# Spreading the queries' reciprocals over their heads' rows: sixteen matmuls with a 0/1 matrix, or transfers through DRAM

## The chip, the cores and the metric

The kernel runs on one core of a Trainium2 chip. The core has a matrix engine (TensorE, PE in the profile), a vector engine (VectorE, DVE), a scalar engine (ScalarE, ACT), GpSimd (POOL) and SyncE (SP). Each engine works through its own list of instructions in order and waits on semaphores where it needs another's result. Transfers are issued here by SP and POOL (a few by ACT) and run on sixteen shared DMA engines. SBUF is the on-chip memory of 128 partitions; PSUM holds what PE writes.

The metric is the device time of one launch in microseconds (us), as the median of several runs. Before the change it is 2350.26 us, the median of 3 runs from 2349.44 to 2350.53.

## The reference

Two branches read the same input `x` of 2048 rows by 512, and a sigmoid gate mixes them. Branch A is linear attention with 32 heads of 16 columns. Branch B is a mixture of eight experts; all eight are taken, each weighted by a softmax.

```python
def _A_ref(x, wqkv, wo):
    H = 32; Dh = D // H
    ...
    phi = lambda t: jnp.where(t > 0, t + 1, jnp.exp(t)) + 1e-6
    pq, pk = phi(q), phi(k)
    kv = jnp.einsum("bhsd,bhse->bhde", pk, v)
    z = jnp.einsum("bhsd->bhd", pk)
    num = jnp.einsum("bhqd,bhde->bhqe", pq, kv)
    den = jnp.einsum("bhqd,bhd->bhq", pq, z)[..., None] + 1e-6
    o = num / den
    return ... o.reshape(B, S, D) @ wo

def _B_ref(x, w_gate, w1, w2):
    ...
    for e in range(E):
        h = _silu(xf @ w1[e]) @ w2[e]
        out = out + w * h

g = _sigmoid((x * gate_w).sum(-1, keepdims=True))
return g * a + (1 - g) * b
```

What matters here is `den`: one sum for each query and head. Each of the 16 columns of a head in `pq` is divided by it. The kernel divides `pq` ahead of the product with `kv`, and folds the gate `g` into the same factor.

## The kernel before, in words

**Tiling.** A value is held as a high and a low float32r part, and a product is three matmuls (`mm3`, lines 57 to 60: high by high, high by low, low by high). The large products go through seven smaller ones each (a Strassen-like scheme), named P1 to P7. The rows come in two halves `h` of 1024, and each half in two blocks `j` of 512 columns. A tile is 128 partitions by 512.

**Parts and ticks.** `m.parts` (line 112) lists the parts in the order in which their second products run: eight experts of the first half, four of the second, the attention's output projection of the first half (`A[0]`), four more experts of the second half, and the attention's second half (`A[1]`). The main loop, `for u in range(LAG + NTICK)` (line 1096), runs one *tick* per turn. In a tick PE does six matmuls of the first products for group `g` (`up`) and six of the second products, `LAG` = 58 ticks behind (`tick(n)` with `n = u - LAG`), so a tick is twelve matmuls of 128x512. The position in a group is `k`, 0 to 6. Everything else is hung into the ticks by hand: each engine's list is in the order in which this loop emits it.

**Order inside a tick.** `other()` comes ahead of the first products and emits preparation of weights, the low halves of hidden tiles (up to three ticks ahead of their matmuls), their high halves, and `queries_first`. `mid()` comes behind the first products and emits `tick(n)` and `queries_last`. The sums `s<-c` (line 690, at k = 5) and `s<-a` (line 696, at k = 6) on DVE empty the PSUM banks `c` and `a`. PSUM tag `a` has two banks; at k = 0 of the next group one of them gets the new `a`, while the old one gets one more product (`a<-n6h`, k = 1).

**The queries' passes.** `m.beside` (line 123) names four parts, and beside each of them one pass `i` runs, for half `h` and block `j` with `h, j = divmod(i, 2)`. Its step `s` is the tick counted from the part's start.

- s = -3, `queries_load`: for even `i` a raw tile `az` is taken, which holds `z` (the keys' sums by head), `spread` (the 0/1 matrix) and `un` (two 128x512 places). SP loads `zcd`, `spd` and the four 128x512 tiles of `pq` (DRAM `pqd`).
- s = 0 to 3: ACT and DVE split each `pq` tile into `un`; PE multiplies by `z` into PSUM `dn`, which gives the 32 sums of each query.
- s = 4 to 9: the high and low sums are added, DVE takes reciprocals in four pieces, and multiplies by the gate (line 982). `Q.r` is 32 x 512.
- s = 10: ACT and DVE split `Q.r` into 64 rows of `un` (lines 984 and 985). POOL has set the rest to zero (line 977).
- s = 14 to 17: PE multiplies by `spread`, one matmul per tile (line 1000), into PSUM `n` with tag `a`; this repeats each head's row over its 16 partitions.
- s = 15 to 18: DVE multiplies each `pq` tile by it (line 988), and SP stores it (line 989).

The matrix `spread` is built on POOL early in the kernel (`bands`, t = 7, lines 438 to 444) and kept in DRAM as `spd`.

Of the kernel before, what the change touches and what calls it, by code (L numbers as in the profile page):

```python
# [10 lines left out]
F32 = mybir.dt.float32  # L11
F32R = mybir.dt.float32r
AF = mybir.ActivationFunctionType
ALU = mybir.AluOpType
AX = mybir.AxisListType

P = 128
S = 2048
D = 512
F = 1792  # L20
E = 8
DH = 16
NH = D // DH
KT = D // P
TB = 512
# [12 lines left out]
def f32(ap):  # L38
    return ap.bitcast(F32)


@with_exitstack
def gated_mix_kernel(ctx: ExitStack, tc: tile.TileContext, xT, x, wk, wv, wqkv_q, wo, wm, out):
    nc = tc.nc
    PS = bass.MemoryType.PSUM

    const = ctx.enter_context(tc.tile_pool(name="const", bufs=1))
    xpool = ctx.enter_context(tc.tile_pool(name="xpool", bufs=14))
    w1p = ctx.enter_context(tc.tile_pool(name="w1p", bufs=1))
    psum = ctx.enter_context(tc.tile_pool(name="psum", bufs=1, space=PS))  # L50
    dram = ctx.enter_context(tc.tile_pool(name="dram", bufs=1, space=bass.MemoryType.DRAM))
    ctx.enter_context(tc.manual_schedule())

    m = SimpleNamespace(nc=nc, tc=tc, const=const, xpool=xpool, w1p=w1p, psum=psum, v=nc.vector,
                        xT=xT, x=x, wk=wk, wv=wv, wq=wqkv_q, wo=wo, wm=wm, out=out)

    def mm3(ps, wh, wlo, xh, xl, start, stop):
        nc.tensor.matmul(ps, wh, xh, start=start, stop=False, skip_group_check=True)  # L58
        nc.tensor.matmul(ps, wh, xl, start=False, stop=False, skip_group_check=True)  # L59
        nc.tensor.matmul(ps, wlo, xh, start=False, stop=stop, skip_group_check=True)  # L60

    def act_copy(dst, src, scale=1.0, bias=0.0):
        nc.scalar.activation(dst, src, AF.Copy, scale=scale, bias=bias)  # L63

    def ps_tile(name, tag, bufs=None):
        return psum.tile([P, TB], F32, name=name, tag=tag, bufs=bufs or {"a": 2, "b": 1, "c": 1, "dn": 4}[tag])

    m.mm3, m.act_copy, m.ps_tile = mm3, act_copy, ps_tile


    def phi_first(dst, src):
        nc.scalar.activation(dst, src, AF.Exp)
        nc.scalar.activation(src, src, AF.Relu)

    def phi_last(dst, src):
        nc.vector.scalar_tensor_tensor(dst, dst, 1.0, src, op0=ALU.min, op1=ALU.add)

    def phi(dst, src):
        phi_first(dst, src)
        phi_last(dst, src)  # L80

    def eps_high(h, d):
        act_copy(h, d, bias=EPS)

    def eps_low(lo, d, h):
        nc.vector.scalar_tensor_tensor(lo, d, EPS, f32(h), op0=ALU.add, op1=ALU.subtract)

    m.phi, m.phi_first, m.phi_last, m.eps_high, m.eps_low = phi, phi_first, phi_last, eps_high, eps_low
    m.ident = const.tile([P, P], F32, name="ident")


    def x_tile(name, tag="x"):
        return xpool.tile([P, 2, TB], F32R, name=name, tag=tag, bufs=14 if tag == "x" else 2)

    m.x_tile = x_tile
    m.XO = [[None] * 7, [None] * 7]
    m.xstash = dram.tile([7, 2, P, 2 * TB], F32, name="xstash")
    m.w2stash = [dram.tile([P, 2, D], F32, name=f"w2stash{i}") for i in range(7 * (E * NPAIR + 2) // 2)]
    m.wgtd = dram.tile([E + 1, S], F32, name="wgtd")
    m.acct = dram.tile([2, 2, KT, P, TB], F32, name="acct")  # L100
    m.pqd = dram.tile([2, 2, KT, P, TB], F32, name="pqd")
    m.wpd = [dram.tile([P, D], F32, name=f"wpd{c}") for c in range(KT)]
    m.zcd = dram.tile([P, KT * 2 * NH], F32, name="zcd")
    m.spd = dram.tile([P, KT * P], F32, name="spd")

    X = [[SimpleNamespace(e=e, h=h, n=NPAIR) for e in range(E)] for h in range(2)]
    A = m.A = [SimpleNamespace(e=E, h=h, n=2) for h in range(2)]
    M = E // 2  # L110

    m.parts = [*X[0], *X[1][:M], A[0], *X[1][M:], A[1]]
    at = 0
    for part in m.parts:
        part.t0, at = at, at + 7 * part.n
    m.NTICK = at
    m.groups = [(part, q) for part in (A[0], *X[0], *X[1][:M], A[1], *X[1][M:]) for q in range(part.n)]
    m.NG = len(m.groups)
    for part in m.parts:
        part.gs = [g for g, (p, _) in enumerate(m.groups) if p is part]  # L120
    m.G1 = X[1][0].gs[0]

    m.beside = [*X[1][:2], *X[1][M:M + 2]]

    misc = ExitStack()
    m.misc = misc.enter_context(tc.tile_pool(name="misc", bufs=1, side="right"))


    def pad(pool):
        nc.gpsimd.memset(pool.tile([P, 24], F32, name="pad", tag="pad", bufs=1), 0.0)  # L130

    m.pad = pad
    weights(m)
    keys(m)
    experts(m, misc)


# [181 lines left out]
def keys(m):  # L319
# [106 lines left out]
    def band(t, pattern, channel):  # L426
        nc.gpsimd.memset(t, 1.0)
        nc.gpsimd.affine_select(out=t, in_=t, compare_op=ALU.is_ge, fill=0.0, base=0,
                                pattern=pattern, channel_multiplier=channel)
        nc.gpsimd.affine_select(out=t, in_=t, compare_op=ALU.is_ge, fill=0.0, base=DH - 1,  # L430
                                pattern=[[-a, n] for a, n in pattern], channel_multiplier=-channel)

    def bands(t):
        if t == 5:
            band(mask.rearrange("p (b e) -> p b e", e=DH), [[-DH, P // DH], [0, DH]], 1)
        elif t == 6:
            band(maskh, [[P, KT], [-DH, NH]], 1)
        elif t == 7:

            spread = m.w1p.tile([P, 2, D], F32, name="spread", tag="ws", bufs=2)[:, 0]  # L440
            nc.gpsimd.memset(spread[2 * NH:], 0.0)
            for i in range(2):
                band(spread[i * NH:(i + 1) * NH].rearrange("p (c f) -> p c f", c=KT), [[P, KT], [1, P]], -DH)
            nc.gpsimd.dma_start(m.spd, spread)

    pk = {}

# [130 lines left out]
def experts(m, misc):  # L578
# [369 lines left out]

    Q = SimpleNamespace()

    def queries_load(i):
        if i % 2 == 0:
            Q.az = m.raw_tile(f"az{i}", F32R)
            Q.z = Q.az[:, :2 * KT * NH].rearrange("p (c f) -> p c f", c=KT)
            Q.spread = Q.az[:, 2 * KT * NH:2 * KT * NH + D].rearrange("p (c f) -> p c f", c=KT)
            Q.un = Q.az[:, 2 * KT * NH + D:2 * KT * NH + 3 * D].rearrange("p (j t) -> p j t", j=2)
            nc.sync.dma_start(f32(Q.az[:, :2 * KT * NH]), m.zcd)
            nc.sync.dma_start(f32(Q.az[:, 2 * KT * NH:2 * KT * NH + D]), m.spd)  # L960
        Q.d = m.raw_tile(f"pq{i}").rearrange("p (c t) -> p c t", c=KT)
        for c in range(KT):
            nc.sync.dma_start(Q.d[:, c], m.pqd[i // 2, i % 2, c])

    def queries_first(i, s):
        h, j = divmod(i, 2)
        if 0 <= s < KT:
            m.eps_high(Q.un[:, 0], Q.d[:, s])
            m.eps_low(Q.un[:, 1], Q.d[:, s], Q.un[:, 0])
        elif s == 4:  # L970
            r = Q.r = out_tile(f"r{i}")[:NH]
            Q.gate = out_tile(f"rg{i}")[:NH]
            at = (2 * h + j) * TB
            nc.sync.dma_start(Q.gate, m.wgtd[E:E + 1, at:at + TB].to_broadcast([NH, TB]))
            act_copy(r, Q.ps[NH:2 * NH], bias=EPS)
            v.tensor_add(r, Q.ps[:NH], r)
            nc.gpsimd.memset(f32(Q.un[2 * NH:, 0]), 0.0)
        if 5 <= s < 9:
            r = Q.r[:, (s - 5) * P:(s - 4) * P]
            v.reciprocal(r, r)  # L980
        elif s == 9:
            v.tensor_mul(Q.r, Q.r, Q.gate)
        elif s == 10:
            act_copy(Q.un[:NH, 0], Q.r)
            v.tensor_sub(Q.un[NH:2 * NH, 0], Q.r, f32(Q.un[:NH, 0]))
        if 15 <= s < 15 + KT:
            d = Q.d[:, s - 15]
            v.scalar_tensor_tensor(d, d, EPS, Q.ps, op0=ALU.add, op1=ALU.mult)
            nc.sync.dma_start(m.pqd[h, j, s - 15], d)

    def queries_last(i, s):
        if 0 <= s < KT:
            if s == 0:
                Q.ps = ps_tile(f"dn{i}", "a")
            for j in range(2):
                nc.tensor.matmul(Q.ps[:2 * NH, :], Q.z[:, s], Q.un[:, j], start=(s == 0 and j == 0),
                                 stop=(s == KT - 1 and j == 1))
        elif 14 <= s < 14 + KT:
            Q.ps = ps_tile(f"n{i}_{s}", "a")
            nc.tensor.matmul(Q.ps, Q.spread[:, s - 14], Q.un[:, 0], start=True, stop=True)  # L1000


    def load_query(part, i):
# [227 lines left out]
```

## Time and profile before

| | |
|---|---|
| median of 3 runs | 2350.26 us (2349.44 to 2350.53) |
| the profiled execution, its own time | 2350.77 us |
| its span, first to last instruction | 2349.1 us |
| mean granted clock of PE | 0.999 |
| DMA, mean over the span | 218 GB/s, 513.23 MB |
| HBM read, written | 343.43 MB, 163.52 MB |

The profile is of one execution. A row of a group gives the source line, the engine, the operation, the tile written and the tiles read, the shapes and the count, and then the duration in ns as least, median and greatest, with the start of the first and the last instruction. A row of the timeline begins with the start and the duration in us; brackets at its end give the idle time before it and what ended that. "A <- B: x, y, z" in a list of waits says that A waited for B for x us in total, y times, at most z. PEld is the load of a matmul's stationary operand, which overlaps the matmuls. Line numbers are those of the kernel before.

### The profile page before, as it was taken

What the parts mean: (1) busy time and instruction counts of PE and PEld (TensorE: products, weight loads), DVE (VectorE), ACT (ScalarE), POOL (GpSimd) and SP (SyncE); (2) the same over time, 40 slices, a digit from 0 to 9 for tenths busy, and PEclk for the clock granted to TensorE, in tenths of its full rate; (3) what the DMA queues carried; (4) which work ended last, traced back from release to release, by engine and by line L of the source; (5) the groups of instructions that cost most, each with busy time, mean ns of one, the idle gap of its engine ahead of it and who ended that gap; (6) DMA issues with size and microseconds to landing.
All of it is one profiled execution on the core that took longest, in us unless ns stands there. A gap on an engine that the chain in (4) does not pass through costs nothing.

```text
span 2349.1 us, 31301 instructions
## 1 busy us (share of the span) xinstructions
PE 2338.4 (100%) x10492; PEld 1935.4 (82%) x10492; DVE 1811.9 (77%) x3102; ACT 1419.3 (60%) x2655; POOL 158.7 (7%) x222
## 2 busy tenths in 40 slices
PE   9999999999999999999999999999999999999999
PEld 8877888888888888888888888888888888888887
DVE  6798888888888888888677768776676777766666
ACT  6686666666666656666555555555565655555553
POOL 2101000000000000000000000000011000000101
PEclk9999999999999999999999999999999999999999
DMA  7898888988889898988845455654556655555566
GB/s 225 239 311 249 264 288 249 278 263 267 268 267 275 256 290 252 271 269 262 287 144 170 152 172 153 182 186 144 163 166 188 182 150 174 162 166 166 165 220 207
DMA packets 299345, 513.23 MB, mean 218 GB/s; under 512 B 24352, under 2 KB 193840, under 8 KB 298800
## 3 DMA queue, kind: packets, MB, share of 16 engines
q1 hardware_dynamic: 274992, 464.10, 59.8%
q0 software_dynamic: 23344, 46.49, 10.8%
q8 instruction: 82, 1.34, 0.2%
q10 hardware_dynamic: 848, 0.66, 0.1%
q14 instruction: 79, 0.65, 0.1%
HBM read 343.43 MB, written 163.52 MB: 216 GB/s over the span
## 4 chain that ended last, share of the span: by engine, by line
PE 97%; DVE 1%; DMA 1%; issue 0%; ACT 0%; POOL 0%; DVEq 0%; ACTq 0%; POOLq 0%
PE p L58 16%; PE p L60 16%; PE p L59 16%; PE a L58 8%; PE a L60 8%; PE a L59 8%; PE c L59 4%; PE c L58 4%; PE c L60 4%; PE b L60 2%; PE b L59 2%; PE b L58 2%; PE g L451 2%; DMA w2stash<-w 1%; PE y L58 1%; PE y L60 1%
## 5 line engine op out<-in xcount | busy, mean ns | idle before, releaser
L58 PE MATMUL p<-ho,w 128*128 128x512 f32 x1620 | 631.4, 390 | 0.8 <-DVE d L844 0.6
L60 PE MATMUL p<-ho,w 128*128 128x512 f32 x1620 | 630.3, 389 | 0.0
L59 PE MATMUL p<-ho,w 128*128 128x512 f32 x1620 | 630.3, 389 | 0.0
L760 DVE TENSOR_TENSOR ho<-s,ho 128x512 fp32r<-128x512 f32 x784 | 537.2, 686 | 71.2 <-ACT ho L63 67.6
L63 ACT ACTIVATE ho<-s 128x512 fp32r<-128x512 f32 x784 | 487.3, 623 | 21.0 <-PE p L60 8.5
L58 PEld LDWEIGHTS p<-ho,w 128*128 128x128 f32 x1620 | 304.0, 188 | 66.7 <-ACT p L63 1.8
L60 PEld LDWEIGHTS p<-ho,w 128*128 128x128 f32 x1620 | 304.2, 188 | 63.2
L59 PEld LDWEIGHTS p<-ho,w 128*128 128x128 f32 x1620 | 304.1, 188 | 63.0
L63 ACT ACTIVATE o<-rs 128x512 fp32r<-128x512 f32 x224 | 129.1, 576 | 172.7 <-PE a L60 111.7
L690 DVE TENSOR_TENSOR s<-c,s 128x512 f32<-128x512 f32 x116 | 80.2, 692 | 188.6 <-PE c L60 178.7
L63 ACT ACTIVATE o<-rm 128x512 fp32r<-128x512 f32 x240 | 137.5, 573 | 99.8 <-PE a L60 77.4
L63 ACT ACTIVATE s<-a 128x512 f32<-128x512 f32 x116 | 69.5, 599 | 146.9 <-PE a L60 140.3
L63 ACT ACTIVATE ws<-rm 128x512 fp32r<-128x512 f32 x203 | 114.7, 573 | 66.2 <-DMA w2stash<-ws 59.3
L619 ACT ACTIVATE s<-s 128x512 f32<-128x512 f32 x224 | 138.7, 619 | 9.9 <-DVE s L696 6.6
L619 ACT ACTIVATE s<-b 128x512 f32<-128x512 f32 x112 | 67.2, 600 | 112.4 <-PE b L60 100.3
L205 DVE TENSOR_TENSOR o<-rm,o 128x512 fp32r<-128x512 f32 x180 | 122.9, 683 | 0.1
L205 DVE TENSOR_TENSOR o<-rs,o 128x512 fp32r<-128x512 f32 x168 | 114.5, 681 | 0.6 <-ACT o L63 0.6
L219 DVE TENSOR_TENSOR ws<-rm,ws 128x512 fp32r<-128x512 f32 x154 | 105.5, 685 | 0.5 <-ACT ws L63 0.5
L696 DVE TENSOR_TENSOR s<-a,s 128x512 f32<-128x512 f32 x116 | 80.0, 689 | 32.8 <-PE a L60 32.5
L63 ACT ACTIVATE b<-a 128x512 f32<-128x512 f32 x116 | 67.1, 579 | 58.1 <-PE a L60 58.0
L63 ACT ACTIVATE s<-c 128x512 f32<-128x512 f32 x116 | 69.0, 595 | 25.6 <-PE c L60 25.6
L815 POOL DMA_DIRECT2D acct<-c x30 | 25.6, 854 | 794.8 <-DVE c L809 779.8
(321 smaller groups left out, 4540.5 us busy)
## 6 DMA issues: line engine op xcount, KB each, us to landing
w<-w2stash SPq DMA_DIRECT2D x403, 512.0 KB, 4.0
w2stash<-ws SPq DMA_DIRECT2D x357, 256.0 KB, 4.2
rm<-wm SPq DMA_DIRECT2D x228, 256.0 KB, 5.2
rs<-wm SPq DMA_DIRECT2D x108, 256.0 KB, 4.0
wb<-wgtd SPq DMA_DIRECT2D x16, 512.0 KB, 5.2
acct<-c POOLq DMA_DIRECT2D x30, 256.0 KB, 5.6
acct<-d POOLq DMA_DIRECT2D x30, 256.0 KB, 5.5
acct<-k POOLq DMA_DIRECT2D x30, 256.0 KB, 5.5
```

The costliest lines, as they stand in the source:

```text
L58: nc.tensor.matmul(ps, wh, xh, start=start, stop=False, skip_group_check=True)
L59: nc.tensor.matmul(ps, wh, xl, start=False, stop=False, skip_group_check=True)
L60: nc.tensor.matmul(ps, wlo, xh, start=False, stop=stop, skip_group_check=True)
L63: nc.scalar.activation(dst, src, AF.Copy, scale=scale, bias=bias)
L205: v.tensor_sub(two(o, 1), src, f32(two(o, 0)))
L219: v.tensor_sub(two(w, 1), src, f32(two(w, 0)))
L451: nc.tensor.matmul(ps, xk((0, 0, 1)[j], tb, k, tt * P, (tt + 1) * P), gw[g][:, (0, 1, 0)[j], k, :], start=(k == 0 and j == 0), stop=(k == ...
L619: nc.scalar.activation(dst, src, AF.Silu)
L690: v.tensor_add(sn[g, 2], bank[g, "c"], sn[g, 2])
L696: v.tensor_add(sn[g, 3], bank[g, "a"], sn[g, 3])
L760: v.tensor_sub(h[1], s, f32(h[0]))
L815: nc.gpsimd.dma_start(m.acct[part.h, j, dt], s, accum_op=ALU.add)
```

## The change

The sixteen matmuls with the 0/1 matrix go, and with them the matrix, its DRAM tensor, the split of `Q.r`, and the memset. In their place `Q.r` is written to a DRAM tensor `rd` by POOL at s = 9, and at s = 10 POOL issues three loads that read each head's row 16 times into 16 partitions. Tile c of the four needs heads 8c to 8c + 7. The loads go into a fresh place `more` of `az` and into the two places of `un`; the fourth goes into `more` again, issued at s = 15 behind the multiplication that reads the first. DVE's multiplications at s = 15 to 18 read these places instead of PSUM.

```diff
-    m.spd = dram.tile([P, KT * P], F32, name="spd")
+    m.rd = dram.tile([2, 2, NH, TB], F32, name="rd")
...
-        elif t == 7:
-
-            spread = m.w1p.tile([P, 2, D], F32, name="spread", tag="ws", bufs=2)[:, 0]
-            nc.gpsimd.memset(spread[2 * NH:], 0.0)
-            for i in range(2):
-                band(spread[i * NH:(i + 1) * NH].rearrange("p (c f) -> p c f", c=KT), [[P, KT], [1, P]], -DH)
-            nc.gpsimd.dma_start(m.spd, spread)
...
-            Q.spread = Q.az[:, 2 * KT * NH:2 * KT * NH + D].rearrange("p (c f) -> p c f", c=KT)
-            Q.un = Q.az[:, 2 * KT * NH + D:2 * KT * NH + 3 * D].rearrange("p (j t) -> p j t", j=2)
+            Q.un = Q.az[:, 2 * KT * NH:2 * KT * NH + 2 * D].rearrange("p (j t) -> p j t", j=2)
+            more = Q.az[:, 2 * KT * NH + 2 * D:2 * KT * NH + 3 * D]
+            Q.by = [f32(t) for t in (more, Q.un[:, 0], Q.un[:, 1], more)]
             nc.sync.dma_start(f32(Q.az[:, :2 * KT * NH]), m.zcd)
-            nc.sync.dma_start(f32(Q.az[:, 2 * KT * NH:2 * KT * NH + D]), m.spd)
...
+        def spread(c):
+            heads = m.rd[h, j, c * P // DH:(c + 1) * P // DH]
+            nc.gpsimd.dma_start(Q.by[c], heads[:, None, :].to_broadcast([P // DH, DH, TB]))
...
-            nc.gpsimd.memset(f32(Q.un[2 * NH:, 0]), 0.0)
...
         elif s == 9:
             v.tensor_mul(Q.r, Q.r, Q.gate)
+            nc.gpsimd.dma_start(m.rd[h, j], Q.r)
         elif s == 10:
-            act_copy(Q.un[:NH, 0], Q.r)
-            v.tensor_sub(Q.un[NH:2 * NH, 0], Q.r, f32(Q.un[:NH, 0]))
+            for c in range(KT - 1):
+                spread(c)
         if 15 <= s < 15 + KT:
             d = Q.d[:, s - 15]
-            v.scalar_tensor_tensor(d, d, EPS, Q.ps, op0=ALU.add, op1=ALU.mult)
+            v.scalar_tensor_tensor(d, d, EPS, Q.by[s - 15], op0=ALU.add, op1=ALU.mult)
             nc.sync.dma_start(m.pqd[h, j, s - 15], d)
+            if s == 15:
+                spread(KT - 1)
...
-        elif 14 <= s < 14 + KT:
-            Q.ps = ps_tile(f"n{i}_{s}", "a")
-            nc.tensor.matmul(Q.ps, Q.spread[:, s - 14], Q.un[:, 0], start=True, stop=True)
```

## The prediction

> **What bounds the kernel now.** I read first the page's head, its clock row and the chain that ended last.
>
> ```profile
> span 2349.1 us, 31301 instructions
> PE 2338.4 (100%) x10492; PEld 1935.4 (82%) x10492; DVE 1811.9 (77%) x3102; ACT 1419.3 (60%) x2655; POOL 158.7 (7%) x222
> PEclk9999999999999999999999999999999999999999
> PE 97%; DVE 1%; DMA 1%; issue 0%; ACT 0%; POOL 0%; DVEq 0%; ACTq 0%; POOLq 0%
> ```
>
> The last row is the point: TensorE (PE) carries 97% of the chain, and its clock is granted throughout. The busy share alone proves little, because the matmuls overlap. So I asked next what PE waited for over the whole span, and how much work each engine has in the stretches where the changed code runs (four passes, near 1260, 1400, 1840 and 1980 us).
>
> ```profile
> PE a L58 <- DVE s L696: 3.9, 2, 3.2
> PE idle L515 <- POOL ones L423: 1.4, 1, 1.4
> PE p L58 <- DVE d L844: 0.6, 1, 0.6
> ```
> ```profile
> 400.00:600.00 200.00, 200.00 (x884) 165.62 (x883) 168.98 (x281) 128.01 (x242) 11.86 (x14) 1.00 0.89 269
> 1300.00:1312.00 12.00, 12.00 (x55) 9.94 (x54) 10.51 (x19) 6.64 (x13) 0.00 (x0) 1.00 0.48 168
> 1420.00:1440.00 20.00, 20.00 (x90) 16.56 (x89) 15.76 (x28) 12.85 (x24) 0.00 (x0) 1.00 0.32 107
> 1860.00:1880.00 20.00, 20.00 (x90) 16.56 (x89) 15.73 (x30) 13.06 (x24) 0.00 (x0) 1.00 0.40 132
> 2000.00:2020.00 20.00, 20.00 (x90) 16.55 (x89) 15.21 (x28) 13.02 (x25) 0.00 (x0) 1.00 0.39 122
> ```
>
> All waits of PE add up to 5.9 us, and none names a tile of the change. The columns of the second fence are the stretch, its length, then busy time and count of PE, weight loads, DVE, ACT and POOL, the clock, the DMA share and GB/s. PE is full in each stretch, with a matmul every 200/884 = 0.226 us; DVE and ACT have room, POOL does nothing, and the DMA engines are less than half used. So a PE instruction taken from one of these passes should shorten the whole program by its place in the stream, and work on other engines is free until it makes PE wait.
>
> **The change: PE's part.** Sixteen products (`n<-az`, four in each of four passes) go.
>
> ```profile
> L1000 PE MATMUL n<-az x16: 389/389/389, 1300.4 to 2022.5; 128*128 128x512 f32 x16
> L988 DVE SCALAR_TENSOR_TENSOR pq<-pq,n x16: 678/682/689, 1301.4 to 2023.8; 128x512 f32<-128x512 f32 x16
> L63 ACT ACTIVATE az<-r x4: 615/615/615, 1287.2 to 2000.5; 32x512 fp32r<-32x512 f32 x4
> L985 DVE TENSOR_TENSOR az<-r,az x4: 680/681/682, 1287.9 to 2001.1; 32x512 fp32r<-32x512 f32 x4
> L977 POOL MEMSET az<- x4: 521/521/521, 1270.5 to 1983.8; 64x512 f32 x4
> L86 DVE SCALAR_TENSOR_TENSOR az<-pq,az x16: 683/692/693, 1259.4 to 1981.2; 128x512 fp32r<-128x512 f32 x16
> ```
> ```profile
> 1300.19 0.39 PE L60 MATMUL p<-ho,w 128*128 128x512 f32 x1
> 1300.42 0.39 PE L1000 MATMUL n<-az 128*128 128x512 f32 x1
> 1300.65 0.39 PE L58 MATMUL b<-n2h,o 128*128 128x512 f32 x1
> 1303.37 0.39 PE L1000 MATMUL n<-az 128*128 128x512 f32 x1
> ```
>
> A product shows 0.389 us, but the next matmul starts 0.23 us after it, as in the rest of the stream. Its price on the path is that distance: 16 x 0.226 = 3.62 us. The bounds are zero (another engine would have held PE anyway) and these 3.62 us; 16 x 0.389 = 6.2 us is no bound, since the overlap isn't given back. I take 3.62: there is no gap before or behind the products. In the order in which the two programs' instructions stand, these 16 are all that PE's stream loses, and nothing changes places around them. The Trainium skill's page "TensorE: Matmul & The Clock Gate" (section "Wait — 56ns, not 53.3ns?") gives 215.7 ns from start to start for 512 columns at full clock; by it the sum would be 3.45 us. The trace's distance is longer, and the trace decides.
>
> **What goes from other engines.** Each pass loses a 0.615 us copy on ACT, a 0.681 us subtraction on DVE and a 0.52 us memset on POOL. PE's full stream covers them (DVE is busy 15 to 16 us of 20 there), so they are worth nothing; uncovered they would bring at most 4 x (0.615 + 0.681) = 5.2 us. At the start POOL no longer builds the matrix of zeros and ones.
>
> ```profile
> 50.99 0.52 POOL L441 MEMSET spread<- 64x512 f32 x1
> 56.51 0.60 POOL L444 DMA_DIRECT2D spd<-spread  x1 [0.30 <-POOL spread L430]
> ```
> ```profile
> 187.82 0.70 PE L58 MATMUL a<-t6h,o 128*128 128x512 f32 x1 [3.15 <-DVE s L696]
> ```
>
> That is 6 us of POOL and one 256 KB write, while PE doesn't wait; zero. The nearest wait of PE behind it is the 3.15 us one above, 130 us later. SP loses two loads of the matrix; also zero. The multiplications that read `n` read SBUF instead of PSUM: the nearest row, L86, has both sources in SBUF and takes 0.692 against 0.682 us, 0.16 us in sum on DVE, covered by PE.
>
> **What is added: two transfers in a row ahead of DVE.** Per pass POOL writes the 32 x 512 reciprocals to DRAM, waits for that to land, and issues three loads of 256 KB that repeat each row for 16 partitions. The fourth load goes into the first one's place, so it is issued only after the first multiplication. The clock of the first pass, in the rows of before:
>
> ```profile
> 1284.82 0.67 DVE L982 TENSOR_TENSOR r<-r,rg 32x512 f32<-32x512 f32 x1
> 1301.38 0.68 DVE L988 SCALAR_TENSOR_TENSOR pq<-pq,n 128x512 f32<-128x512 f32 x1
> 1308.17 0.69 DVE L690 TENSOR_TENSOR s<-c,s 128x512 f32<-128x512 f32 x1 [0.74 <-PE c L60]
> 1310.59 0.68 DVE L988 SCALAR_TENSOR_TENSOR pq<-pq,n 128x512 f32<-128x512 f32 x1
> 1311.18 0.68 DVE L696 TENSOR_TENSOR s<-a,s 128x512 f32<-128x512 f32 x1
> ```
> ```profile
> 1314.93 0.39 PE L58 MATMUL a<-n6h,o 128*128 128x512 f32 x1
> ```
> ```profile
> L1012 POOL DMA_DIRECT2D q<-pqd x16: 538/768/885, 1724.7 to 2246.0; - x16
> DMA to landing us min/median/max: 3.6/5.0/7.0
> ```
> ```profile
> DMA to landing us min/median/max: 3.7/5.6/9.3
> ```
> ```profile
> pqd<-s POOLq DMA_DIRECT2D x8, 256.0 KB, 4.0
> pqd<-e POOLq DMA_DIRECT2D x8, 256.0 KB, 4.9
> n4h<-xstash SPq DMA_DIRECT2D x1, 512.0 KB, 11.4
> ```
>
> The first landing row is of `q<-pqd`, the nearest kind: 256 KB loads from DRAM issued by POOL. The second is of POOL's 120 accumulating stores to `acct`. The last fence has POOL's plain stores of 256 KB and the longest landing of any issue. No row is of a load that repeats rows in this form, so I bound its landing, and the write's, at L = 3.6 and 11.4 us. I take 5.0 for the load (nearest row) and 4.5 for the write (between the two stores). Then: the reciprocals are ready at 1284.82 + 0.67 = 1285.5, the write lands at 1290.0, and the first load at 1295.0, 6.4 us before its use at 1301.38; the next two are issued 0.77 us apart and used 2.7 us apart, so they are safer. The fourth is issued at 1301.38 + 0.68 = 1302.06, lands at 1307.1, and is due at 1310.59, less the 0.9 us by which PE then runs ahead (four products): 1309.7, 2.6 us to spare. The other passes have the same spacing: the last use lies 25.8 us after the product with the gates in the first pass, and the group rows' ends (2023.8, and 1998.1 for the last `r<-r,rg`) give 25.7. So DVE doesn't wait, and the price is zero.
>
> ```profile
> 1437.51 0.68 DVE L988 SCALAR_TENSOR_TENSOR pq<-pq,n 128x512 f32<-128x512 f32 x1
> ```
> ```profile
> 1452.25 0.85 POOL L815 DMA_DIRECT2D acct<-c  x1 [45.07 <-DVE c L809]
> ```
>
> What stands behind the waits: on POOL nothing until the store of `c`, in the second pass 14 us after the end of the first multiplication, which issues the fourth load. On DVE, behind a late multiplication, stand the low halves of the hidden tiles (three ticks of 12 matmuls ahead of theirs, 3 x 12 x 0.226 = 8 us) and, behind the fourth, L696, which frees bank `a` for PE's matmul at 1314.93. On SP the store of each product and weight loads issued some five ticks early. The tightest is L696: it ends 1.28 us after the fourth multiplication starts and is due at 1314.93 - 0.9 = 1314.0, so that multiplication may start as late as 1312.7. With L above 7.9 us for both steps it starts at 1285.5 + 2L + 0.68 + L, which meets 1312.7 at L = 8.85 us. From there each us of L costs 3 us a pass, 12 in four.
>
> A rule of the Trainium skill speaks against these loads: "DMA: Bandwidth & Descriptors", section "Rules for kernel authors", says that an outermost dimension smaller than 16 confines a transfer to that many engines, and the source here has 8 heads outermost. At the 168 / 0.48 = 350 GB/s of the second windows row, 256 KB are 0.75 us on sixteen engines and 1.5 on eight, so by the rule an estimated landing of 5.8, still under 7.6; the sum stays, the slower rival gains a little. No row of before shows such a transfer.
>
> Bytes: 4 x 1.05 MB are added and 0.8 MB go, of 513 MB, in stretches at a DMA share below one half.
>
> **Sum.** -3.62 + 0 = -3.62 us. From the profiled execution's own time (2350.77: span 2349.1 and 1.7 around it) that gives 2347.15. This execution lies 0.51 us above the median of the runs (2350.26), so against the median I forecast 2346.64, 0.15% less.
>
> **Rivals.**
> 1. Slower: the two transfers land late. One mechanism, at bank `a` in the seventh tick, deciding from L = 8.85 us for write and load alike; the gain is eaten at 9.15, and 0.2% lost at 9.54. At 9.3 us it gives 12 x 0.45 - 3.6 = +1.8, 2352.0; at 11.4, 12 x 2.55 - 3.6 = +27, 2377. For it: the fourth load has only 2.6 us to spare for DVE. Against: medians of 4.0 to 5.6, idle POOL, quiet DMA engines.
> 2. The products were hidden anyway: DVE sets the pace in those four ticks (10.51 of 12 us busy), and PE waits as long as it saves: 2350.3. Against: its 19 instructions follow each other at 0.60 us, 11.4 us as an upper reckoning against 51 x 0.226 = 11.5 for PE, and it still waited 0.74 us for PE there.
> 3. More than forecast: POOL's six us and its write at the start, once gone, loosen the 3.15 us wait at 187.82: 2346.64 - 3.15 = 2343.5. For it: it is PE's largest wait. Against: the write landed near 62 us, and PE was full between.
>
> **How the numbers follow.** Forecast 0.78, first rival 0.08, second 0.04, third 0.10. A change under 0.2% (4.70 us, bounds 2345.56 and 2354.96) is about what a measurement of this kernel can't tell from none. The forecast lies inside it; the runs of before reach 0.82 us below and 0.27 above their median, so I put 0.04 of its 0.78 below 2345.56. Faster: 0.10 + 0.04 = 0.14. Slower: the first rival from 9.54 us, 0.06. Same: 0.80. The range goes from 2346.64 less 0.82, moved 0.8 further towards the third rival (2345.0), to 2349.4, where late landings or a held PE have taken three quarters of the gain.
>
> **What would show it.** Right: 16 fewer PE matmuls, the four stretches still full with starts 0.226 us apart, no wait of PE on `a` or of DVE on a load of `rd`, landings of `rd` under 7.6 us, and everything behind the last pass some 3.6 us earlier. Rival 1: DVE's multiplication waits for a DMA, and PE's `a` for DVE L696's counterpart. Rival 2: the same PE gaps with no DMA named. Rival 3: the wait near 187 us shrinks. A gain apart from 2.9 to 4.4 us with none of these signs would make my price of a matmul wrong.

## The result, and the profile after

| | before | changed |
|---|---|---|
| median | 2349.66 us (2348.02 to 2350.97, 15 runs) | 2345.11 us (2343.78 to 2346.30, 15 runs) |
| ratio of the runs | | 0.998, 95% interval 0.9973 to 0.9987 |
| the profiled execution, its span | 2349.1 us | 2344.2 us |

The changed kernel is faster by 4.55 us. That is 0.19%, just inside the 0.2% that I had set as the line, but the interval, 3.1 to 6.3 us, leaves "no change" out. The forecast was 3.62 us, which the interval holds: the times alone do not tell 4.55 from 3.62. In each fence below the lines are those of the changed kernel, whose line numbers differ a little: L987 is the multiplication that was L988, L980 the product with the gates (L982), and L683 and L689 the sums that were L690 and L696.

The page's head, and the whole list of what PE waited for:

```profile
span 2344.2 us, 31276 instructions
PE 2334.6 (100%) x10476; PEld 1932.3 (82%) x10476; DVE 1808.9 (77%) x3098; ACT 1418.7 (61%) x2651; POOL 165.1 (7%) x230
PE 96%; DVE 2%; DMA 1%; issue 0%; ACT 0%; SPq 0%; POOL 0%; ACTq 0%; POOLq 0%
```
```profile
PE a L58 <- DVE s L689: 3.1, 2, 2.4
PE idle L508 <- POOL ones L423: 1.4, 1, 1.4
PE p L58 <- DVE d L837: 0.6, 1, 0.6
```

PE has 16 matmuls fewer, 10476 for 10492, and the same three waits as before. Two are unchanged. The first has shrunk from 3.9 to 3.1 us in sum, and its longest case from 3.2 to 2.4. No wait names a transfer of the change.

The timeline of PE at the first product's old place, and the same passes as before by stretches (length, then busy time and count of PE, weight loads, DVE, ACT and POOL, then clock, DMA share, GB/s):

```profile
1299.21 0.39 PE L60 MATMUL p<-ho,w 128*128 128x512 f32 x1
1299.44 0.39 PE L58 MATMUL b<-n2h,o 128*128 128x512 f32 x1
...
1313.04 0.39 PE L58 MATMUL a<-n6h,o 128*128 128x512 f32 x1
```
```profile
1300.00:1312.00 12.00, 12.00 (x55) 9.93 (x54) 11.29 (x20) 6.43 (x12) 0.59 (x1) 1.00 0.62 200
1860.00:1880.00 20.00, 20.00 (x90) 16.57 (x89) 15.08 (x28) 12.94 (x24) 2.99 (x5) 1.00 0.65 200
2000.00:2020.00 20.00, 20.00 (x90) 16.57 (x89) 15.82 (x28) 12.28 (x23) 0.59 (x1) 1.00 0.71 209
```

The matmul of bank `b` now follows the last of `p` directly, and PE is as full as before. The DMA share in the passes went from 0.39 to 0.48 up to 0.62 to 0.71, which disturbs nobody there.

POOL's and DVE's timelines in the first pass, then the group row of the loads with the landings of write and loads together:

```profile
1284.80 0.55 POOL L981 DMA_DIRECT2D rd<-r  x1 [26.05 <-DVE r L980]
1287.94 1.83 POOL L964 DMA_DIRECT2D az<-rd  x3 [2.59 <-DMA rd<-r]
1301.38 0.59 POOL L964 DMA_DIRECT2D az<-rd  x1 [11.61 <-DVE pq L987]
```
```profile
1283.83 0.67 DVE L980 TENSOR_TENSOR r<-r,rg 32x512 f32<-32x512 f32 x1
1300.40 0.69 DVE L987 SCALAR_TENSOR_TENSOR pq<-pq,az 128x512 f32<-128x512 f32 x1
1308.92 0.69 DVE L987 SCALAR_TENSOR_TENSOR pq<-pq,az 128x512 f32<-128x512 f32 x1
1309.52 0.69 DVE L689 TENSOR_TENSOR s<-a,s 128x512 f32<-128x512 f32 x1
```
```profile
L964 POOL DMA_DIRECT2D az<-rd x16: 587/607/652, 1287.9 to 2011.9; - x16
...
DMA to landing us min/median/max: 2.4/4.4/7.5
```

The write lands in about 2.6 us and the loads are issued at 1287.94, some 12 us ahead of their first use. Neither multiplication shown has an idle time in brackets, and in DVE's list of waits over the four passes no load of `rd` stands: DVE waits for none. The fourth load is issued at 1301.38 and due at 1308.92, 7.5 us later; read one at a time, the four fourth loads landed in 4.0, 6.3, 4.4 and 6.4 us. So the spare time was 1.1 us in two of the passes.

**Where the 4.9 us of the two profiled executions went.** Follow one matmul through both traces. The one behind the long wait starts at 187.82 before and 187.06 now, 0.76 us earlier. The first `b<-n2h` behind a product starts at 1300.65 before and 1299.44 now: 1.21, of which 0.23 are that product, so 0.98 came earlier. The last store is issued by SP at 2345.65 before and 2341.06 now, 4.59: between lie 3.61 us for the sixteen products, 0.226 each. The last 0.3 us of the span are the landing of that store. So the products brought what they were priced at, and 0.98 us came in at places where the changed code does not run: 0.76 at the long wait, and 0.22 between 1150 and 1160 us, at matmuls `p<-ho,w`, where neither list has a wait. The larger part is followed up here. These are the stretches around it, first before and then after:

```profile
180.00:190.00 10.00, 6.85 (x26) 5.27 (x25) 6.79 (x11) 5.91 (x12) 0.00 (x0) 0.90 0.66 216
190.00:200.00 10.00, 10.00 (x43) 8.18 (x42) 7.38 (x18) 7.46 (x16) 0.00 (x0) 0.93 0.92 269
```
```profile
180.00:190.00 10.00, 7.59 (x30) 5.86 (x29) 7.54 (x13) 6.67 (x14) 0.00 (x0) 0.89 0.70 232
190.00:200.00 10.00, 10.00 (x43) 8.23 (x42) 7.59 (x18) 7.07 (x15) 0.00 (x0) 0.94 0.86 263
```
```profile
187.06 0.50 PE L58 MATMUL a<-t6h,o 128*128 128x512 f32 x1 [2.41 <-DVE s L689]
```

The wait is 2.41 us instead of 3.15, and four more matmuls fit into the first ten microseconds. The experiments ask whether that belongs to the change.

### The profile page after: what moved, and what is told of

It is laid out like the page before. It is cut to its first block, busy times and chain, and to the rows that moved or that the text cites. A ratio compares the mean times of both kernels' runs of the same rounds, so it can differ in the third digit from the quotient of the medians.

```text
span 2344.2 us, 31276 instructions
## 1 busy us (share of the span) xinstructions
PE 2334.6 (100%) x10476; PEld 1932.3 (82%) x10476; DVE 1808.9 (77%) x3098; ACT 1418.7 (61%) x2651; POOL 165.1 (7%) x230
## 4 chain that ended last, share of the span: by engine, by line
PE 96%; DVE 2%; DMA 1%; issue 0%; ACT 0%; SPq 0%; POOL 0%; ACTq 0%; POOLq 0%
PE p L58 16%; PE p L60 15%; PE p L59 15%; PE a L58 8%; PE a L60 8%; PE a L59 8%; PE c L58 4%; PE c L59 4%; PE c L60 4%; PE b L60 2%; PE b L58 2%; PE b L59 2%; PE g L444 2%; PE y L58 1%; PE y L60 1%; PE y L59 1%
## 5 line engine op out<-in xcount | busy, mean ns | idle before, releaser
L683 DVE TENSOR_TENSOR s<-c,s 128x512 f32<-128x512 f32 x116 | 80.2, 692 | 193.5 <-PE c L60 180.6
L689 DVE TENSOR_TENSOR s<-a,s 128x512 f32<-128x512 f32 x116 | 80.0, 690 | 33.7 <-PE a L60 33.4
L716 DVE TENSOR_TENSOR s<-s,s 128x512 f32<-128x512 f32 x112 | 76.8, 686 | 0.0
```

Source lines behind the costliest of these rows:

```text
L683: v.tensor_add(sn[g, 2], bank[g, "c"], sn[g, 2])
L689: v.tensor_add(sn[g, 3], bank[g, "a"], sn[g, 3])
L716: v.tensor_sub(t21, t21, t11)
```

## The experiments

Fifteen runs: twelve new kernels, one of them a second time under another name, and the kernel before and the changed one once more. "Medians" below stand against the median of the kernel before taken on the same chip in the same group of runs. A ratio is given with its interval as recorded; it is not the quotient of the two medians, and differs from it by up to 0.0004.

### The price of a product

The kernel before a second time (`e0`), and with each product issued twice (`e1`).

```diff
             Q.ps = ps_tile(f"n{i}_{s}", "a")
-            nc.tensor.matmul(Q.ps, Q.spread[:, s - 14], Q.un[:, 0], start=True, stop=True)
+            for _ in range(2):
+                nc.tensor.matmul(Q.ps, Q.spread[:, s - 14], Q.un[:, 0], start=True, stop=True)
```

> The kernel before, a second time: what two equal kernels differ by. Theory 1 (the gain is 16 places of 0.2266 us in PE's stream, 3.62 us; what the two profiled executions differ by beyond that, 0.75 us in PE's wait near 186 us, is scatter of that wait): ratio 1.000 within 0.0005, and the wait near 186 us lies anywhere from 2.4 to 3.2 us. Theory 2 (the early work on POOL belongs to the gain: it lengthens the wait near 186 us): ratio 1.000 too, but the wait is 3.1 to 3.2 us again.

> The kernel before with each of the 16 products issued twice. Theory 1: each costs its place in PE's stream, so +16 x 0.2266 = +3.6 us, ratio 1.0015. Rival (the products are hidden behind DVE in their ticks): 0 to +1 us, ratio 1.000. Wait near 186 us as in the kernel before (theory 2: 3.1 to 3.2 us).

The second run of the kernel before gave 2350.19 against 2350.55 us, ratio 1.0002 (0.9993 to 1.0011). With 32 products it was 2354.14 us, ratio 1.0014 (1.0005 to 1.0023): 3.59 us for sixteen more, 0.224 each. PE's timeline of that kernel, at the first pair:

```profile
1299.91 0.39 PE L60 MATMUL p<-ho,w 128*128 128x512 f32 x1
1300.14 0.62 PE L1001 MATMUL n<-az 128*128 128x512 f32 x2
1300.59 0.39 PE L58 MATMUL b<-n2h,o 128*128 128x512 f32 x1
```

Two products hold the stream for 0.45 us. The path pays the distance between starts, 0.226, not the 0.389 that a row shows, and the rival that DVE hides the products is out.

### The transfers

First they are left out altogether (`e3`); DVE then multiplies by what lies in `un`, so the division is left out too.

```diff
-            nc.gpsimd.dma_start(m.rd[h, j], Q.r)
...
-            for c in range(KT - 1):
-                spread(c)
...
-            Q.by = [f32(t) for t in (more, Q.un[:, 0], Q.un[:, 1], more)]
+            Q.by = [f32(Q.un[:, c % 2]) for c in range(KT)]
```

> The changed kernel without the write of the reciprocals and without the loads; DVE multiplies by what lies in the two places of the split queries, so the division of branch A is left out. Theory 1: the transfers cost nothing, so the time is that of the changed kernel, -3.6 us, ratio 0.9985. Rival (the transfers take part of the gain through the DMA engines): 0.5 us or more below the changed kernel, ratio 0.998 or less.

2346.29 against 2350.55 us, ratio 0.9985 (0.9976 to 0.9994), and a span of 2344.3 us where the changed kernel has 2344.2. The transfers cost nothing that can be seen.

Then they are made late. In `e4` the fourth load goes to the third one's place and so waits for the third multiplication; in `e5` all loads share one place.

```diff
-            Q.by = [f32(t) for t in (more, Q.un[:, 0], Q.un[:, 1], more)]
+            Q.by = [f32(t) for t in (more, Q.un[:, 0], Q.un[:, 1], Q.un[:, 1])]
...
-            if s == 15:
+            if s == 17:
                 spread(KT - 1)
```
```diff
+            Q.by = [f32(more)] * KT
...
+            spread(0)
...
+            if s - 14 < KT:
+                spread(s - 14)
```

> The changed kernel, its fourth load sent to the place of the third, so that it is issued behind the third multiplication instead of the first, one tick and a half later. Worked out on the changed kernel's first pass: issue at 1305.14 + 0.68 + 0.3 = 1306.1 us, landing 4.0 to 6.4 us later as its fourth loads did, due at 1308.9. Theory 1 (DVE may be late, since PE needs bank a only at 1313.04, and DVE's sum ends 1.28 us after the multiplication starts): DVE waits 1 to 4 us a pass for the load, PE waits not at all in passes with a landing up to 5.6 us and up to 0.8 us in the others; time 0 to 1.6 us above the changed kernel, ratio 0.9985 to 0.9992. Rival (a wait of DVE goes straight to PE): 5 to 14 us above it, ratio 1.0005 or more.

> The changed kernel with one place for all four loads, so that each waits for the multiplication of the tile before. Theory 1, with a landing of 4.4 us: the fourth multiplication starts at 1300.4 + 3 x (0.69 + 0.3 + 4.4) = 1316.6 us, its sum frees bank a at 1317.9, and PE, due at 1313.04, waits 4.8 us a pass, 19 us in four; with 6.4 us it waits 10.8, 43 in four; a few us more if the granted clock drops behind the waits. Ratio 1.006 to 1.017, PE's waits named bank a behind DVE's sum. Rival (DVE's other work, ahead by three ticks, keeps PE fed and bank a is not the tight place): ratio 1.002 or less, or PE's wait is named p and not a.

`e4`: 2347.27 against 2350.17 us, ratio 0.9987 (0.9978 to 0.9996). The list of waits, then DVE and PE in the second pass:

```profile
DVE pq L987 <- DMA az<-rd: 9.1, 4, 3.3
```
```profile
1446.91 0.69 DVE L987 SCALAR_TENSOR_TENSOR pq<-pq,az 128x512 f32<-128x512 f32 x1 [3.25 <-DMA az<-rd]
1447.52 0.68 DVE L689 TENSOR_TENSOR s<-a,s 128x512 f32<-128x512 f32 x1
```
```profile
1448.26 0.50 PE L58 MATMUL a<-n6h,o 128*128 128x512 f32 x1 [0.41 <-DVE s L689]
```

DVE now waits 9.1 us in four passes, and PE passes on about a tenth of it. Its waits on `a` grew by two, 0.41 us here and 0.49 in the fourth pass, the two with the long landings; in the other two passes it does not wait for `a`. The end of the sum L689 at 1448.20 is followed at once by PE's `a<-n6h`. That is the tight place named beforehand, met at its edge.

`e5`: 2382.1 against 2350.17 us, ratio 1.0135 (1.012 to 1.0151). The waits of PE and of DVE, DVE and PE in the first pass, and the stretch around it:

```profile
PE a L58 <- DVE s L689: 29.5, 6, 7.6
```
```profile
DVE pq L986 <- DMA az<-rd: 40.2, 12, 4.9
```
```profile
1317.17 0.69 DVE L986 SCALAR_TENSOR_TENSOR pq<-pq,az 128x512 f32<-128x512 f32 x1 [3.52 <-DMA az<-rd]
1317.78 0.68 DVE L689 TENSOR_TENSOR s<-a,s 128x512 f32<-128x512 f32 x1
```
```profile
1318.52 0.80 PE L58 MATMUL a<-n6h,o 128*128 128x512 f32 x1 [5.45 <-DVE s L689]
1319.11 0.63 PE L59 MATMUL a<-n6l,o 128*128 128x512 f32 x1
1319.54 0.63 PE L60 MATMUL a<-n6h,o 128*128 128x512 f32 x1
```
```profile
1312.00:1324.00 12.00, 6.55 (x18) 4.93 (x17) 7.76 (x13) 4.13 (x8) 0.14 (x1) 0.74 0.59 176
```

The fourth multiplication starts at 1317.17; 1316.6 was worked out. PE waits 5.45 us for bank `a` here and more in passes with slower landings, 26 us in four. Behind each wait its matmuls start 0.43 us apart instead of 0.23 and the granted clock of the stretch is 0.74. So late transfers do what the slower rival said, in the place it named. And waits of this length cost more than themselves: the span is 37 us longer than the changed kernel's (2381.5 against 2344.2) for 26 us of added waits.

Last, whether 8 rows outermost slow a load. In `e6` each load reads all 32 rows four times, so the factors are spread over the wrong heads and the right division is left out.

```diff
-            heads = m.rd[h, j, c * P // DH:(c + 1) * P // DH]
-            nc.gpsimd.dma_start(Q.by[c], heads[:, None, :].to_broadcast([P // DH, DH, TB]))
+            nc.gpsimd.dma_start(Q.by[c], m.rd[h, j][:, None, :].to_broadcast([NH, P // NH, TB]))
```

> The changed kernel, each load reading all 32 rows four times instead of 8 rows sixteen times, so that the outermost dimension of its source is 32 and not 8; the factors are spread wrongly, so the division of branch A is left out of what is right. It asks whether 8 outermost rows slow a load. If they do (half of the engines): landings 0.5 to 1 us shorter than the changed kernel's (four first loads 3.9 to 5.0 in the quiet first pass, median of all rows 4.4). If not: the same within 0.3 us. Time as the changed kernel either way, ratio 0.998 to 0.9985, since no load is waited for.

2346.3 against 2350.4 us, ratio 0.9984 (0.9975 to 0.9993): no difference in time is seen. The landings differ. The clearest are the fourth loads, which are issued alone: in nine profiles of kernels with 8 rows outermost they took 4.0 to 4.5 us in the first pass, 6.2 to 6.7 in the second, 4.1 to 4.7 in the third and 6.2 to 6.4 in the fourth; with 32 rows 2.9, 4.4, 3.0 and 4.6. The first three loads, issued together, show less of it: in the first pass 4.0 to 4.1 us against 3.9 to 6.7. The Trainium skill's rule ("DMA: Bandwidth & Descriptors", section "Rules for kernel authors": an outermost dimension under 16 confines a transfer to that many engines) agrees in direction, with 1.1 to 2.3 us as the difference here. My estimate from it was 0.75. How many engines a load used is not shown, and the edit changes a second thing: a row is read four times instead of sixteen. No run parts the two.

### The wait near 186 us

Three edits of the changed kernel put back parts of the early work: all of it, unread (`e2`); the building without the store (`e7`); a store of zeros without the building (`e8`).

```diff
+        elif t == 7:
+            spread = m.w1p.tile([P, 2, D], F32, name="spread", tag="ws", bufs=2)[:, 0]
+            ...
+            nc.gpsimd.dma_start(m.spd, spread)
```
```diff
+        elif t == 7:
+            nc.gpsimd.dma_start(m.spd, f32(zero))
```

> The changed kernel with the matrix of zeros and ones built and stored at the start again, and read by nobody. Theory 1: as the changed kernel, -3.6 us against the kernel before, ratio 0.9985, wait near 186 us anywhere from 2.4 to 3.2 us. Theory 2: the wait near 186 us is 3.1 to 3.2 us again, and the gain is smaller than that of the changed kernel by 0.8 to 1 us.

> The changed kernel with the matrix built on POOL in its old place at the start, but not stored. It tells what of the early work lengthens the wait near 186 us (3.1 to 3.5 us in four kernels with it, 2.4 and 2.7 us in two without). If the building or the tile's place in the ring does: wait 3.1 to 3.5 us, ratio 0.9988. If the store does: 2.4 to 2.7 us, ratio 0.9985 or less. If the six waits fell so by chance: anything from 2.4 to 3.5 us.

> The changed kernel with a store of 256 KB by POOL at the place of the old one, from the tile of zeros that lies in SBUF anyway; nothing is built. If the store lengthens the wait near 186 us: 3.1 to 3.5 us, ratio 0.9988. If the building or the tile's place does: 2.4 to 2.7 us, ratio 0.9985 or less. By chance: anything from 2.4 to 3.5 us.

Then two such stores (`e11`), one store by SP (`e12`, `nc.sync` in place of `nc.gpsimd`), and the changed kernel a second time (`e15`).

> The changed kernel with two stores of 256 KB by POOL near 50 us, of zeros, instead of none. Five kernels with one such store waited 3.1 to 3.5 us near 186 us, five without 2.0 to 2.7. If the bytes are what counts: 3.9 to 4.4 us. If any store changes a state that then stays: 3.1 to 3.5 us. If the number matters only in its phase: 2.0 to 2.7 us.

> The changed kernel with one store of 256 KB near 50 us, of zeros, issued by SP instead of POOL. If the bytes of the store lengthen the wait near 186 us: 3.1 to 3.5 us. If POOL's queue does: 2.0 to 2.7 us.

> The changed kernel a second time: wait near 186 us 2.0 to 2.7 us as in six kernels without an early store, ratio 0.9980 to 0.9985.

PE's wait for DVE's sum near 186 us in the profile of each kernel, in us:

| early store of 256 KB | the wait, one profile each |
|---|---|
| one, by POOL | 3.15 (before), 3.50 (`e0`), 3.06 (`e1`), 3.30 (`e2`), 3.41 (`e8`) |
| none | 2.41 (changed), 2.69 (`e3`), 2.50 (`e4`), 2.26 (`e5`), 2.02 (`e6`), 2.04 (`e7`), 2.41 (`e15`) |
| two, by POOL | 2.60 (`e11`) |
| one, by SP | 2.90 (`e12`) |

| | median | before, same group | ratio (interval) |
|---|---|---|---|
| `e2`, all put back | 2347.26 | 2350.55 | 0.9985 (0.9976 to 0.9994) |
| `e8`, store alone | 2346.59 | 2350.17 | 0.9983 (0.9974 to 0.9992) |
| `e7`, building alone | 2345.64 | 2350.17 | 0.9981 (0.9972 to 0.9989) |
| `e11`, two stores | 2346.53 | 2350.40 | 0.9984 (0.9975 to 0.9994) |
| `e12`, by SP | 2346.37 | 2350.40 | 0.9985 (0.9976 to 0.9994) |
| `e15`, changed again | 2345.90 | 2350.40 | 0.9982 (0.9974 to 0.9991) |

The five waits with one POOL store and the seven without any do not overlap, and with the building alone (`e7`) the wait is as short as without. Two lines of the timelines, of `e8` and of `e7`:

```profile
187.77 0.50 PE L58 MATMUL a<-t6h,o 128*128 128x512 f32 x1 [3.41 <-DVE s L692]
```
```profile
186.74 0.50 PE L58 MATMUL a<-t6h,o 128*128 128x512 f32 x1 [2.04 <-DVE s L695]
```

What ends the wait stands in ACT's timeline, first of the kernel before and then of the changed one:

```profile
185.21 0.63 ACT L63 ACTIVATE wx<-rm 128x512 fp32r<-128x512 f32 x1 [3.46 <-DMA w2stash<-wx]
```
```profile
184.44 0.63 ACT L63 ACTIVATE wx<-rm 128x512 fp32r<-128x512 f32 x1 [2.72 <-DMA w2stash<-wx]
```

ACT prepares a weight tile, and waits for a store of prepared weights that SP issued near 179 us; DVE waits for ACT, and PE for DVE. In the five profiles with one POOL store this copy starts at 185.16 to 185.46 us, in the seven without at 184.08 to 184.53; SP's store landed in 5.5 to 6.0 us in the five and in 4.8 to 5.4 in the seven.

So the early store that the change drops goes with 0.95 us of this wait (the means are 3.28 and 2.33), through a later landing of SP's store, though it was itself issued more than 120 us earlier. How, stays open. More bytes do not mean a longer wait, since two stores gave 2.60; the 2.90 with SP lies between the two groups and decides nothing. Each of these kernels with an early store also has that store's tensor in DRAM, and no run has the one without the other.

Nor is chance ruled out. Each wait is that of one execution. Without the pair that raised the question, ten waits remain, and chance would give the four longest of ten to the four kernels with the store once in 210 times. But executions of one kernel lie up to 4.4 us apart (`e1`, 2351.10 to 2355.52), and only 0.9 to 1.6 us once this wait is taken out (below), so the wait may well differ by more than 0.95 us between executions of one kernel. The medians point the same way (with one POOL store 3.3 and 3.6 us below the kernel before, without 4.5, 4.5 and, in `e3` and `e6`, 4.3 and 4.1), but their intervals overlap, and the ratios of `e2` and `e8` came out lower than the 0.9988 expected of the store.

### The same comparison without the wait

The place that ACT waits for is that of a spare tile: the third prepared tile of the group at tick 54 takes a place in a ring of two. If the ring is taken up one tick later, the first two tiles of that group come from the larger ring and the third finds a free place.

```diff
-        m.spare = ho_tile if u < LAG - 8 else xs_tile if u < LAG - 1 else None
+        m.spare = ho_tile if u < LAG - 7 else xs_tile if u < LAG - 1 else None
```

> The changed kernel, in which the prepared weights change from one ring of spare tiles to the smaller one a tick later (tick 51 instead of 50), so that the third tile of that group need not wait for the store of the first. It asks what the wait near 186 us costs. If that wait is what it looks like (2.0 to 3.5 us of PE and some 1.4 us of matmuls at half clock behind it): the wait is gone or moved, and the time 2 to 4.5 us below the changed kernel, ratio 0.9965 to 0.9975. Rival (the DMA engines are the bound there, and the wait comes back a group later): ratio 0.998 to 0.9985.

> The kernel before with the spare tiles changed over at tick 51, as in the changed kernel with that edit. Without the wait near 186 us its scatter can't add to or take from the change. If the change is worth its 16 places in PE's stream and the rest came through that wait: this kernel lies 3.6 us above the changed kernel with the same edit, in the traces 3.4 to 4.0 us, and its wait near 186 us is under 1 us too; ratio to the kernel before 0.9985. If the early store or the transfers act elsewhere too: 4.5 us or more, or under 3.

> The changed kernel with the spare tiles changed over at tick 51, a second time, beside the kernel before with the same edit: 3.6 us below that one; ratio to the kernel before 0.997.

On the changed kernel the edit gave 2342.53 us (`e9`, ratio to the kernel before 0.997, 0.9959 to 0.998) and 2342.57 (`e14`, 0.9969, 0.9956 to 0.9981). On the kernel before it gave 2345.91 (`e13`, 0.9982, 0.9973 to 0.9991). PE's timeline and the two stretches of `e9`, then PE's waits on `a` in `e13` and in `e14`:

```profile
184.87 0.50 PE L58 MATMUL a<-t6h,o 128*128 128x512 f32 x1 [0.52 <-DVE s L689]
```
```profile
180.00:190.00 10.00, 9.48 (x42) 7.50 (x41) 8.42 (x15) 6.99 (x14) 0.00 (x0) 1.00 0.83 264
190.00:200.00 10.00, 10.00 (x46) 8.27 (x45) 8.55 (x18) 9.04 (x17) 0.00 (x0) 1.00 0.85 266
```
```profile
PE a L58 <- DVE s L696: 1.2, 2, 0.7
```
```profile
PE a L58 <- DVE s L689: 1.2, 2, 0.7
```

Both kernels now wait the same 1.2 us on bank `a`, and what is left between them is the change: spans of 2344.2 and 2340.6 us, 3.6 apart, and medians 3.34 apart, for 3.62 worked out. In these kernels ACT's copy does not wait for SP's store issued near 179 us, and it landed in 5.5 us with the early store (`e13`), and in 5.2 and 5.7 without (`e9`, `e14`): no effect of the early store shows there. The version with both edits, 7.8 us below the kernel before in that group of runs, beats both kernels.

## Why the prediction was right, and where not

- **The products: right.** Sixteen places of 0.226 us, 3.62 in sum. The trace gives 3.61, doubling them costs 3.59, and without the early wait the traces differ by 3.6.
- **The transfers at zero: right, with less to spare than worked out.** I took 4.5 us for the write and 5.0 for a load. The write took 2.4 to 3.0 (it is a quarter of the size of the rows I took), the fourth loads 4.0 to 6.4. DVE had 1.1 us left in two passes instead of 2.6. The edge at bank `a` holds: `e4` met it and `e5` went past it.
- **The work taken from DVE, ACT and SP at zero, and the source in SBUF: right, as far as shown.** The multiplications took 0.686 us instead of 0.682. PE has no new wait, and 3.6 us are left for the sixteen products; no run puts this work back alone.
- **The line of 0.2%: this step failed.** The prediction took a change under 0.2% as "about what a measurement of this kernel can't tell from none", and so gave 0.80 to no change, against its own sum of 3.62 us faster. Fifteen runs told 0.07% either way: 3.1 to 6.3 us faster, and "no change" is out. The time of 2345.11 us lies at the low end of the range, 2345.0 to 2349.4.
- **The early work at zero: this term of the sum failed too, as far as the profiles show.** The prediction said of it "That is 6 us of POOL and one 256 KB write, while PE doesn't wait; zero." With the building alone the wait is as short as without it, but without the store PE's wait near 186 us is 0.95 us shorter on the average of the profiles, 0.76 in the pair compared. With that wait taken out of both kernels the change is worth 3.34 us by the medians, where it was 4.55 with it. Why an early store should matter there stays open. I had found PE full between store and wait. But the chain that ends in that wait runs through stores of prepared weights, in a phase in which the DMA engines are about 0.9 busy; PE's fullness said nothing of it. The prediction called the DMA engines less than half used; that holds for the four passes, while its own row of 400 to 600 us has them at 0.89.
- **The third rival was half right.** It named this place, but priced the wait as all or nothing (2343.5), with 0.10. A part of it came instead, and 3.62 + 0.95 = 4.57 us lies close to the 0.2% line of 4.70. That this meets the measured 4.55 so closely is partly luck, with an interval of 3.1 to 6.3.

## What to carry to other kernels

Price an instruction of a full engine by the distance to the next start, and check the price by doubling it. For a transfer put in ahead of a consumer, work out which instruction behind the consumer another engine waits for: here DVE could wait 9 us in sum and PE passed on less than one. A change that moves a few transfers early on may go with another wait in a later phase in which the DMA engines are nearly full; to see a change alone, compare the kernels with that wait taken out of both.

## What the runs showed of the hardware that was not expected

A wait of PE of 2 us and more cost more than its length. The granted clock of the two stretches from 180 to 200 us is 0.90 and 0.93 in the kernel before, with a wait of 3.15 us, and 0.90 and 0.93 in `e6`, with 2.02 us: (0.10 + 0.07) x 10 = 1.7 us of lost clock in both. In the other kernels with such a wait the two are shared out otherwise, with the same sum within 0.01; in `e9`, with a wait of 0.52 us, it is 1.00 in both. So taking out 1.9 us of wait brought 3.4 us of span (2344.2 to 2340.8), near the 1.9 + 1.7 = 3.6 of wait and lost clock. The Trainium skill ("TensorE: Matmul & The Clock Gate", section "What's actually happening") puts the drop to half clock behind an idle window of about 3.4 us. Here 2.0 us were enough, and the measurement decides.

A store of 256 KB by POOL, landed long before, went with 0.95 us more, on average, of a wait that another transfer ends, in the five profiles with it against seven without. With two such stores, and where that wait had been taken out, no such effect shows. No run shows the cause, and chance is not ruled out.
